# Three low bits of a narrowed weight: from a shift on VectorE to an activation on ScalarE

## The chip, the core and the metric

The kernel runs on one core of one Trainium2 chip. The metric is device time in microseconds (us) of one execution; lower is better. A core has TensorE (PE, with a separate row PEld for its weight loads), VectorE (DVE), ScalarE (ACT), GpSimd (POOL) and SyncE (SP), each with its own instruction stream that it works through in order. Here SP issues most DMAs, ACT a few, and POOL only sets up constants.

## The reference, cut to what matters

```python
# attention, batch 8, heads 8, 576 rows, head size 64, 32 packed queries
p_packed = sm_attn(p, k, v)               # softmax attention of p over k, v
out = sm_attn(q, p_packed, p_packed)      # q over the packed rows
x = out.transpose(0, 2, 1, 3).reshape(4608, 512)
h = maximum(maximum(x @ w1, x @ w2), x @ w3)   # 512 -> 768
x = h @ w_out                                   # 768 -> 512
h = x @ w_in2                                   # 512 -> 2048
g = maximum(h, 0) + log1p(exp(-abs(h)))
return g @ w_out2                               # 2048 -> 512
```

The weight matrices arrive as 64-bit floats; q, k, v and p arrive as 32-bit floats. The kernel reads each 64-bit number as two 32-bit words, the low word first.

## The kernel before, in words

**Stages.** The program works through eight batches. For each it runs the packed attention (q and k transposed, scores, exponentials, a transposed copy, the value products), then layer 1 (`layer1_unit`, L397: 18 units of 12 matmuls per batch, the maximum over three weights), then layer 2 (`layer2`, L434). The last part (`layer3`, `layer4`, from L814) runs the two large layers over nine chunks of 512 rows. Every fp32 product is made of three matmuls on a high and a low part, which `split` (L105) makes: L106 on ScalarE rounds to the high part, L107 on VectorE subtracts it.

**Narrowing.** A 64-bit weight is brought to fp32 by two helpers. `rebase` (L79) takes the high word as a float and moves its exponent with one ScalarE activation (L82). `narrow` (L90) takes the top three bits of the low word with a VectorE shift in place (L93), and then shifts the rebased bits left by three and ors these bits in (L96, VectorE). It is called 56 times on a tile of 128 x 512: 18 times for the three layer 1 weights (`narrow_w`, tiles `wraw` to `wsb`), 6 times for the layer 2 weight (`split_wo`, tiles `woraw` to `wo32`), and 32 times for the weights of the last two layers (`narrow_ahead`, L639, tiles `raw` to `x32`), which are stored narrowed and read back later. The first 24 stand in the first 105 us; the other 32 are spread over batches 1 to 6, six slots per batch.

**What sets the order.** The first batch is written as a string of step names (L490 to L499), where `LWfw` loads a layer 1 weight, `Nfw` narrows it, `LOf` and `SOf` do the same for the layer 2 weight, `S`, `E`, `Vv`, `PT`, `A` are the steps of the attention, and `PW` is the product of packed rows and weights (`ps_w`, L374). A scheduler then places the instructions of each engine by its own estimate of when their inputs are there, so the order on an engine is not that of the string. In the later batches TensorE's units are chained (`pinned`, L568) and SP's loads too (`in_turn`, L625). The raw weight tiles come from a pool of 5 buffers (`stp`), q and k tiles from a pool of 5 (`rx`), PSUM tiles of the attention stages from a pool of 4 (`mm`). A load of a sixth weight waits until an earlier tile has been narrowed by L96.

**Names used below.** `woraw_204` is the second layer 2 weight tile; `wraw_597` is the eleventh layer 1 weight tile to be loaded. `mx` (L261) is the row maximum of the first scores, `e` (L270) their exponential, `e1T` (L291) the copy of its transpose, `ps_v` (L305) the value products, `pp` (L319) the packed rows that result, `ps_t` (L230) their transpose, `ps_s` (L246) the scores, and `s` (L332) the transposed scores of the second softmax.

Of the kernel before, what the change touches and what calls it, by code (L numbers as in the profile page):

```python
# [11 lines left out]
AF = mybir.ActivationFunctionType  # L12
ALU = mybir.AluOpType
# [6 lines left out]
def packed_attention_maxout_softplus(  # L20
# [22 lines left out]
    nc = tc.nc  # L43
# [46 lines left out]
    def narrow(raw, x):  # L90

        low, bits = raw[:, :, 0], x.bitcast(I32)
        nc.vector.tensor_scalar(  # L93
            out=low, in0=low, scalar1=29, scalar2=None, op0=ALU.logical_shift_right
        )
        nc.vector.scalar_tensor_tensor(  # L96
            out=bits,
            in0=bits,
            scalar=3,
            in1=low,  # L100
            op0=ALU.logical_shift_left,
            op1=ALU.bitwise_or,
        )
# [31 lines left out]
    praw, raw, vt, pT, e1, esum, e1T, pp, ppT = ({} for _ in range(9))  # L135
# [328 lines left out]
    def split_wo(f, t):  # L464
        x = mp.tile([P, S], F32, tag="m", name="wo32")
        rebase(t, x[:, :DM])
        narrow(t, x[:, :DM])
        split(x[:, :DM], wo_hi[:, f], wo_lo[:, f])
# [11 lines left out]
    def narrow_w(f, w, t):  # L480
        x = wsb[:, 3 * f + w].rearrange("p c x -> p (c x)")
        rebase(t, x)
        narrow(t, x)
# [155 lines left out]
    def narrow_ahead():  # L639
        if len(in_flight) == AHEAD or not to_narrow and in_flight:  # L640
            raw64, dst = in_flight.pop(0)
            x = nwp.tile([P, 512], F32, tag="x32", name="x32")
            rebase(raw64, x)
            narrow(raw64, x)
            if len(dst.shape) == 3:
                x = x.rearrange("p (j x) -> p j x", x=P)
            to_store.append((dst, x))
        if to_narrow:
            src, dst = to_narrow.pop(0)
            t = stp.tile([P, 512, 2], I32, tag="st", name="raw64")  # L650
            in_turn(lambda: nc.sync.dma_start(out=t.rearrange("p n t -> p (n t)"), in_=src))
            in_flight.append((t, dst))
# [294 lines left out]
```

## Time and profile before

| | |
|---|---|
| runs without a profile | 1292.54, 1289.27, 1292.12 us; median 1292.12 |
| the profiled execution | 1288.91 us, of which the span from first to last instruction is 1287.1 |
| PE busy | 1250.0 us (97%), 9952 matmuls |
| PEld busy | 1127.7 us (88%) |
| DVE busy | 719.4 us (56%), 1115 instructions |
| ACT busy | 458.2 us (36%), 669 instructions |
| chain that ended last | PE 81%, DVE 2%, DMA 1% of the span |

All times of the profile are of that one execution, counted from its first instruction. Busy shares are means over stages that differ much: PE's row of 40 slices begins 3, 8, 8 and then stays at 9 or more. So the first slices and the rest have to be read apart, and in the first slices what matters is what each engine waited for.

### The profile page before, as it was taken

What the parts mean: (1) busy time and instruction counts of PE and PEld (TensorE: products, weight loads), DVE (VectorE), ACT (ScalarE), POOL (GpSimd) and SP (SyncE); (2) the same over time, 40 slices, a digit from 0 to 9 for tenths busy, and PEclk for the clock granted to TensorE, in tenths of its full rate; (3) what the DMA queues carried; (4) which work ended last, traced back from release to release, by engine and by line L of the source; (5) the groups of instructions that cost most, each with busy time, mean ns of one, the idle gap of its engine ahead of it and who ended that gap; (6) DMA issues with size and microseconds to landing.
All of it is one profiled execution on the core that took longest, in us unless ns stands there. A gap on an engine that the chain in (4) does not pass through costs nothing.

```text
span 1287.1 us, 23495 instructions
## 1 busy us (share of the span) xinstructions
PE 1250.0 (97%) x9952; PEld 1127.7 (88%) x9952; DVE 719.4 (56%) x1115; ACT 458.2 (36%) x669; POOL 0.7 (0%) x6
## 2 busy tenths in 40 slices
PE   3889999999999999999999999999999999999998
PEld 2679898998989899999999999999999999999997
DVE  3777777786857657686354443544434445444332
ACT  3553434444343434553323323232232222332221
POOL 0000000000000000000000000000000000000000
PEclk7899999999999999999999999999999999999999
DMA  9972848677685724977646556565465554654651
GB/s 263 240 212 91 204 136 231 174 212 193 185 231 171 201 87 166 343 257 266 225 172 225 187 208 214 187 215 212 180 208 203 205 205 172 228 188 180 213 182 58
DMA packets 82121, 255.10 MB, mean 198 GB/s; under 512 B 12128, under 2 KB 47200, under 8 KB 72544
## 3 DMA queue, kind: packets, MB, share of 16 engines
q1 hardware_dynamic: 76240, 242.46, 59.1%
q10 hardware_dynamic: 5776, 11.14, 2.5%
q8 instruction: 78, 1.28, 0.4%
q14 instruction: 27, 0.22, 0.1%
HBM read 211.62 MB, written 41.94 MB: 197 GB/s over the span
## 4 chain that ended last, share of the span: by engine, by line
PE 81%; DVE 2%; DMA 1%; issue 0%; ACT 0%; SPq 0%; DVEq 0%
PE ps L812 28%; PE ps L395 21%; PE acc L860 10%; PE acc L859 10%; PE acc L858 10%; PE ps_w L374 2%; DMA wc<-wic 1%; PE ps_v L305 1%; PE ps_e L285 1%; DVE pwlo L107 1%; DVE mx L261 0%; PE ps_s L246 0%; DVE m L420 0%; DVE x L96 0%; DMA qraw<-in_q_dram 0%
## 5 line engine op out<-in xcount | busy, mean ns | idle before, releaser
L812 PE MATMUL ps<-x2hi,wc 128*128 128x256 f32 x2016 | 370.6, 282 | 0.8 <-DMA wc<-wic 0.8
L812 PEld LDWEIGHTS ps<-x2hi,wc 128*128 128x128 f32 x2016 | 316.1, 190 | 3.9 <-DMA wc<-wic 1.3
L812 PE MATMUL ps<-x2lo,wc 128*128 128x256 f32 x1008 | 283.7, 281 | 0.0
L860 PE MATMUL acc<-w2hi,glo 128*128 128x512 f32 x576 | 224.9, 391 | 0.0
L859 PE MATMUL acc<-w2lo,ghi 128*128 128x512 f32 x576 | 224.8, 390 | 0.0
L858 PE MATMUL acc<-w2hi,ghi 128*128 128x512 f32 x576 | 224.3, 389 | 0.0
L812 PEld LDWEIGHTS ps<-x2lo,wc 128*128 128x128 f32 x1008 | 191.4, 190 | 2.8
L841 ACT ACTIVATE h<-h 128x1024 f32<-128x1024 f32 x72 | 76.3, 1059 | 286.3 <-DVE h L838 286.3
L835 DVE TENSOR_TENSOR h<-h,ps 128x512 f32<-128x512 f32 x72 | 49.5, 687 | 227.8 <-PE ps L812 227.8
L107 DVE TENSOR_TENSOR glo<-h,ghi 128x1024 fp32r<-128x1024 f32 x72 | 88.1, 1223 | 85.1 <-ACT ghi L106 85.0
L395 PE MATMUL ps<-a2hi,pwhi 128*128 128x288 f32 x576 | 129.2, 306 | 2.9 <-DVE pwlo L107 0.9
L860 PEld LDWEIGHTS acc<-w2hi,glo 128*128 128x128 f32 x576 | 108.1, 188 | 23.0 <-DVE glo L107 0.2
L858 PEld LDWEIGHTS acc<-w2hi,ghi 128*128 128x128 f32 x576 | 108.3, 188 | 20.3
L859 PEld LDWEIGHTS acc<-w2lo,ghi 128*128 128x128 f32 x576 | 108.1, 188 | 20.5
L395 PE MATMUL ps<-a2lo,pwhi 128*128 128x288 f32 x576 | 123.8, 297 | 0.3 <-DVE a2lo L107 0.3
L395 PE MATMUL ps<-a2hi,pwlo 128*128 128x288 f32 x576 | 123.6, 296 | 0.0
L395 PEld LDWEIGHTS ps<-a2hi,pwhi 128*128 128x128 f32 x576 | 91.8, 189 | 17.9 <-ACT m L418 5.9
L834 ACT ACTIVATE h<-ps 128x256 f32<-128x256 f32 x72 | 27.5, 382 | 188.0 <-PE ps L812 188.0
L420 DVE TENSOR_TENSOR m<-ps,m 128x576 f32<-128x576 f32 x96 | 72.4, 755 | 38.8 <-PE ps L395 31.4
L395 PEld LDWEIGHTS ps<-a2lo,pwhi 128*128 128x128 f32 x576 | 93.1, 190 | 0.6 <-DVE a2lo L107 0.5
L395 PEld LDWEIGHTS ps<-a2hi,pwlo 128*128 128x128 f32 x576 | 93.0, 190 | 0.2 <-DVE pwlo L107 0.2
L107 DVE TENSOR_TENSOR pwlo<-ps_w,pwhi 128x512 fp32r<-128x512 f32 (+1 forms) x80 | 50.5, 631 | 67.1 <-ACT pwhi L106 66.6
(87 smaller groups left out, 1473.8 us busy)
## 6 DMA issues: line engine op xcount, KB each, us to landing
wc<-wic SPq DMA_DIRECT2D x66, 1792.0 KB
qraw<-in_q_dram SPq DMA_DIRECT2D x112, 140.0 KB
wic<-wc SPq DMA_DIRECT2D x8, 1792.0 KB
kraw<-in_k_dram SPq DMA_DIRECT2D x96, 140.0 KB
wraw<-in_moe_w_dram SPq DMA_DIRECT2D x18, 512.0 KB
x2d<-xs ACTq DMA_DIRECT2D x32, 288.0 KB
xu<-x2d SPq DMA_DIRECT2D x36, 256.0 KB
out_dram<-o SPq DMA_DIRECT2D x136, 64.0 KB
```

The lines of the kernel that those rows point to most:

```text
L107: nc.vector.tensor_tensor(out=lo, in0=src, in1=hi.bitcast(F32), op=ALU.subtract)
L285: nc.tensor.transpose(ps[: 32 * TI, i // hi, (i % hi) * P : (i % hi) * P + P], e[:, i], ident,)
L374: nc.tensor.matmul(ps[cols, G, : units * P].rearrange("p (w x) -> p w x", w=units), ppT[n][rows, cols], wsb[rows, 4 * c : 4 * c + units, g ...
L395: nc.tensor.matmul(o, w, xx, start=first, stop=last)
L420: nc.vector.tensor_tensor(out=m, in0=ps[:, :, :HS], in1=ms[n, f], op=ALU.max)
L812: nc.tensor.matmul(out, l, r, start=(i == 0), stop=(i == len(terms) - 1))
L834: nc.scalar.activation(out=h[:, 3], in_=pa[:, 0], func=AF.Copy)
L835: add(out=h[:, 0:5:4], in0=h[:, 3:4].to_broadcast([P, 2, HC]), in1=pb, op=ALU.add)
L841: nc.scalar.activation(out=g, in_=g, func=AF.Softplus)
L858: nc.tensor.matmul(ps, ghi[:, i, cols], whi, start=first, stop=False)
L859: nc.tensor.matmul(ps, ghi[:, i, cols], wlo, start=False, stop=False)
L860: nc.tensor.matmul(ps, glo[:, i, cols], whi, start=False, stop=last)
```

## The change

In `narrow`, the VectorE shift of the low word by 29 is gone. In its place ScalarE reads the top byte of the low word (every eighth byte of the tile) as an unsigned 8-bit number b, computes b/32 - 31/64, and writes it as a 32-bit integer back to the low word's place. [...] L96 on VectorE then reads the word as before; its other input still comes from L82 on ScalarE.

```diff
     def narrow(raw, x):
 
         low, bits = raw[:, :, 0], x.bitcast(I32)
-        nc.vector.tensor_scalar(
-            out=low, in0=low, scalar1=29, scalar2=None, op0=ALU.logical_shift_right
-        )
+        top = raw.bitcast(mybir.dt.uint8)[:, :, 3]
+        nc.scalar.activation(out=low, in_=top, func=AF.Copy, scale=1.0 / 32, bias=-31.0 / 64)
         nc.vector.scalar_tensor_tensor(
             out=bits,
```

56 VectorE instructions leave and 56 ScalarE instructions (L94 of the changed kernel) come. Every later line of the changed kernel has a number one lower than before (L96 is its L95). Because the scheduler places instructions anew, others move too.

VectorE, around 30 us, between the narrowing of `wraw_199` and of `wraw_211`, before:

```order
L96 SCALAR_TENSOR_TENSOR wsb_114<-wsb_114,wraw_199 128x512
L93 TENSOR_SCALAR woraw_204<-woraw_204 128x512
L261 TENSOR_REDUCE mx_283<-ps_s_265 128x1
L96 SCALAR_TENSOR_TENSOR wo32_255<-wo32_255,woraw_204 128x512
L265 TENSOR_SCALAR ms_285<-mx_283 128x1
L261 TENSOR_REDUCE mx_290<-ps_s_266 128x1
```

The same place of VectorE in the changed kernel:

```order
L95 SCALAR_TENSOR_TENSOR wsb_114<-wsb_114,wraw_199 128x512
L260 TENSOR_REDUCE mx_283<-ps_s_265 128x1
L260 TENSOR_REDUCE mx_290<-ps_s_266 128x1
L95 SCALAR_TENSOR_TENSOR wo32_255<-wo32_255,woraw_204 128x512
L264 TENSOR_SCALAR ms_285<-mx_283 128x1
```

Both maxima now stand ahead of everything that needs the tile `woraw_204`; the scaling of the first maximum (L265, now L264) still stands behind its L96.

ScalarE, at the same place, before (from the rebase of `woraw_204` to the second `e1T`):

```order
L82 ACTIVATE wo32_255<-woraw_204 128x512
L211 ACTIVATE vT_237<-ps_k_238 128x3x3x32 x2
L232 ACTIVATE pT_302<-ps_t_300 128x128
L106 ACTIVATE wo_hi_115<-wo32_255 128x512
L270 ACTIVATE e1_287,es_288<-ps_s_265,ms_285 128x576
L82 ACTIVATE wsb_114<-wraw_211 128x512
L270 ACTIVATE e1_294,es_295<-ps_s_266,ms_292 128x576
L291 ACTIVATE e1T_311<-ps_e_304 96x768
L82 ACTIVATE wsb_114<-wraw_216 128x512
L291 ACTIVATE e1T_323<-ps_e_316 96x768
```

ScalarE there in the changed kernel, from the new instruction on `woraw_204`:

```order
L94 ACTIVATE woraw_204<-woraw_204 128x512
L231 ACTIVATE pT_302<-ps_t_300 128x128
L105 ACTIVATE wo_hi_115<-wo32_255 128x512
L82 ACTIVATE wsb_114<-wraw_211 128x512
L94 ACTIVATE wraw_211<-wraw_211 128x512
L269 ACTIVATE e1_287,es_288<-ps_s_265,ms_285 128x576
L269 ACTIVATE e1_294,es_295<-ps_s_266,ms_292 128x576
L82 ACTIVATE wsb_114<-wraw_216 128x512
L94 ACTIVATE wraw_216<-wraw_216 128x512
L290 ACTIVATE e1T_311<-ps_e_304 96x768
L82 ACTIVATE wsb_114<-wraw_221 128x512
L94 ACTIVATE wraw_221<-wraw_221 128x512
```

The second `e1T` follows directly behind these rows. Four new instructions and two rebases that stood elsewhere are now between the rebase of `woraw_204` and the second `e1T`.

VectorE, around 80 us, where the packed rows `pp` of batch 1 are made, before:

```order
L107 TENSOR_TENSOR hlo_876<-m_828,hhi_875 128x576
L107 TENSOR_TENSOR pwlo_851<-ps_w_852,pwhi_850 128x512
L96 SCALAR_TENSOR_TENSOR wsb_114<-wsb_114,wraw_870 128x512
L319 TENSOR_SCALAR pp_880<-ps_v_879,rc_931 128x64
L107 TENSOR_TENSOR pwlo_851<-ps_w_852,pwhi_850 128x512
L319 TENSOR_SCALAR pp_880<-ps_v_879,rc_936 128x64
L107 TENSOR_TENSOR wo_lo_116<-wo32_943,wo_hi_115 128x512
```

The same place in the changed kernel:

```order
L95 SCALAR_TENSOR_TENSOR wsb_114<-wsb_114,wraw_870 128x512
L106 TENSOR_TENSOR hlo_876<-m_828,hhi_875 128x576
L95 SCALAR_TENSOR_TENSOR wo32_943<-wo32_943,woraw_779 128x512
L106 TENSOR_TENSOR pwlo_851<-ps_w_852,pwhi_850 128x512
L106 TENSOR_TENSOR wo_lo_116<-wo32_943,wo_hi_115 128x512
L318 TENSOR_SCALAR pp_880<-ps_v_879,rc_931 128x64
L318 TENSOR_SCALAR pp_880<-ps_v_879,rc_936 128x64
L106 TENSOR_TENSOR pwlo_851<-ps_w_852,pwhi_850 128x512
```

The first `pp` now stands behind the whole narrowing and splitting of the third layer 2 weight (`woraw_779`), the second no longer behind the second `pwlo`. On SP, the loads of one k tile of batch 1 and of `wraw_597` now stand ahead of the load of v for batch 1 (`vt`), which waits for `ps_v` of batch 0; `wraw_597` stood behind eight loads of q before. On TensorE, in the first two units of layer 1, matmuls of the second unit on the first head group now stand between the two head groups of the first unit. From batch 1 on, the order is the same but for the moved instructions themselves and a few neighbours.

## Rows read from the trace of the kernel before

**Rows 1.** Stretches: us; busy PE, PEld, DVE, ACT, POOL; clock, DMA share, GB/s.
```profile
0.00:57.40 57.40, 33.53 (x533) 24.67 (x533) 27.99 (x57) 25.40 (x48) 0.70 (x6) 0.79 1.02 254
57.40:69.30 11.90, 10.11 (x75) 9.53 (x75) 9.41 (x21) 5.87 (x12) 0.00 (x0) 1.00 0.42 138
69.30:82.60 13.30, 9.26 (x171) 7.21 (x172) 12.60 (x25) 9.12 (x16) 0.00 (x0) 1.00 0.90 250
90.00:515.00 425.00, 422.74 (x4279) 382.09 (x4278) 304.10 (x527) 176.87 (x307) 0.00 (x0) 1.00 0.64 176
515.00:1275.00 760.00, 759.17 (x4825) 690.69 (x4824) 359.88 (x482) 238.10 (x285) 0.00 (x0) 1.00 0.58 207
```

**Rows 2.** PE's longest wait from 90 to 515 us: total, times, longest.
```profile
PE ps L395 <- DVE pwlo L107: 0.9, 5, 0.2
```

**Rows 3.** Groups of one shape: busy us, mean ns | idle before, releaser.
```profile
L93 DVE TENSOR_SCALAR raw<-raw 128x512 int32<-128x512 int32 x32 | 13.2, 413 | 0.0
...
L93 DVE TENSOR_SCALAR wraw<-wraw 128x512 int32<-128x512 int32 x18 | 7.6, 421 | 17.9 <-DMA wraw<-in_moe_w_dram 17.9
...
L93 DVE TENSOR_SCALAR woraw<-woraw 128x512 int32<-128x512 int32 x6 | 2.5, 423 | 2.3 <-DMA woraw<-in_moe_w_out_dram 2.3
...
L82 ACT ACTIVATE wsb<-wraw 128x512 f32<-128x512 f32 x18 | 12.0, 681 | 17.7 <-DMA wraw<-in_moe_w_dram 17.6
...
L106 ACT ACTIVATE wo_hi<-wo 128x512 fp32r<-128x512 f32 x6 | 3.8, 629 | 0.5 <-DVE wo L96 0.5
...
L841 ACT ACTIVATE h<-h 128x1024 f32<-128x1024 f32 x72 | 76.3, 1059 | 286.3 <-DVE h L838 286.3
```

**Rows 4.** Timeline of ACT: start, duration, instruction, count, idle before.
```profile
30.38 0.68 ACT L211 ACTIVATE vT<-ps_k 128x288 f32<-128x288 f32 x2
...
32.06 0.72 ACT L270 ACTIVATE e<-ps_s,ms 128x576 f32<-128x576 f32 x1
...
35.77 0.81 ACT L291 ACTIVATE e1T<-ps_e 96x768 f32<-96x768 f32 x1
```

**Rows 5.** Timeline of ACT from 60 to 70 us.
```profile
64.60 0.65 ACT L418 ACTIVATE m<-ps 128x576 f32<-128x576 f32 x1 [0.78 <-PE ps L395]
65.15 1.23 ACT L82 ACTIVATE wsb<-wraw 128x512 f32<-128x512 f32 x2
```

**Rows 6.** Timeline of DVE from 26 to 37 us.
```profile
29.80 0.43 DVE L93 TENSOR_SCALAR woraw<-woraw 128x512 int32<-128x512 int32 x1 [2.07 <-DMA woraw<-in_moe_w_out_dram]
30.14 0.75 DVE L261 TENSOR_REDUCE mx<-ps_s 128x1 f32<-128x576 f32 x1
30.81 0.68 DVE L96 SCALAR_TENSOR_TENSOR wo<-wo,woraw 128x512 int32<-128x512 int32 x1
```

**Rows 7.** Timeline of DVE from 35 to 46 us.
```profile
38.52 0.48 DVE L319 TENSOR_SCALAR pp<-ps_v,rc 128x64 f32<-128x64 f32 x2 [0.64 <-PE ps_v L305]
...
44.57 1.45 DVE L332 STREAM_TRANSPOSE s<-ps_s 128x576 f32<-128x576 f32 x2 [1.92 <-PE ps_s L246]
```

**Rows 8.** Timeline of PE from 35 to 59 us.
```profile
35.66 2.79 PE L305 MATMUL ps_v<-vt,e1T 96*32 96x64 f32 x96
...
57.41 0.53 PE L395 MATMUL ps<-a2hi,pwhi 128*128 128x288 f32 x2 [0.60 <-ACT a2hi L106]
58.20 0.52 PE L395 MATMUL ps<-a2lo,pwhi 128*128 128x288 f32 x2 [0.27 <-DVE a2lo L107]
```

**Rows 9.** Timeline of PE from 69 to 83 us.
```profile
69.28 1.09 PE L374 MATMUL ps_w<-wsb,ppT 64*32 64x512 f32 x16 [1.52 <-DVE wsb L96]
...
76.93 1.09 PE L374 MATMUL ps_w<-wsb,ppT 64*32 64x512 f32 x16 [0.98 <-DVE wsb L96]
...
82.56 0.30 PE L230 MATMUL ps_t<-ident,pp 128*128 128x128 f32 x1 [3.06 <-DVE pp L319]
```

**Rows 10.** Timeline of SP from 31 to 52 us: issues.
```profile
31.52 0.37 SPq L472 DMA_DIRECT2D wraw<-in_moe_w_dram  x1
38.51 0.33 SPq L169 DMA_DIRECT2D vt<-in_v_dram  x1
```

## The prediction, written before the changed kernel ran

> **What bounds the kernel now.** The table of stretches comes first, because the kernel has two parts. From 90 to 515 us PE is busy 422.74 of 425.00 us, and from 515 to 1275 us 759.17 of 760.00, both at the full granted clock, 1.00 or 2.4 GHz [rows 1]. There PE is the bound. In PE's list of waits for the first of these stretches the largest entry is 0.9 us, in five pieces of at most 0.2 [rows 2]. The 32 narrowings of batches 1 to 6 lie here: whatever they save or cost on other engines, PE hardly waits for them. Before 90 us it is otherwise: up to 57.4 us PE works 33.53 of 57.40 us, while the DMA engines are full (share 1.02); from 57.4 to 69.3 it works 10.11 of 11.90; and from 69.3 to 82.6 only 9.26 of 13.30, while VectorE is busy 12.60 [rows 1]. So the time of the kernel is decided by when PE comes out of this beginning. I then read, in the timelines, each PE wait there: 0.60 and 0.27 us for the split of the second softmax at 57.41 and 58.20 [rows 8], and then 1.52 for a narrowed weight at 69.28, 0.98 for another at 76.93, and 3.06 for the packed rows `pp` at 82.56 [rows 9]. After the last PE never stops for long.
>
> **The change part by part.** Removed: 56 shifts of VectorE, 13.2 + 7.6 + 2.5 = 23.3 us, 0.42 us each [rows 3]. 32 of them (13.2 us) lie beside a PE that is the bound and are worth nothing. 24 (10.1 us) lie before 105 us.
>
> Added: 56 activations of 128 x 512 on ScalarE. No row shows one that reads a byte. The nearest is L82, which reads the same tile in the same step of eight bytes: 681 ns, of which a neighbour behind it overlaps some, two in a row taking 1.23 us or 0.61 each [rows 3, 5]. From below I take 629 ns, the same size read without a step (L106), and from above 1059 ns, an activation of 1024 elements (L841), as if each byte cost two [rows 3]. I take 0.68, or 0.61 in a row, since tile, size and step are those of L82. Could it be a gain? Not on ScalarE, where nothing leaves.
>
> Page rule and row differ a little here. L82 against L106 shows 0.05 us for the step [rows 3]. The Trainium skill (SBUF — State Buffer, the passage on cachelines) says that accesses run at full rate as long as at least two fall on one 16-byte line. A byte from every eight has two, so by it the instruction would take the 629 ns of L106, and the sum below would be 0.5 instead of 1.1 us.
>
> The late part: 32 x 0.61 = 20 us more on ScalarE, which has 176.87 of 425.00 us of work there [rows 1]; what hides it is PE's own work. I put it at nothing. If the cover were gone, as with a copy of `pp` delayed by one instruction, it would cost up to 0.6 us for each of six batches, 3.6 us.
>
> The first place, 30 to 58 us. Before, the first maximum (L261) waits on VectorE behind a shift that waits for the DMA of `woraw_204`, until 29.80 us [rows 6]. The shift gone, the maximum moves ahead by about 2 us. But this gain isn't kept: the scaling of the maximum still stands behind L96 of that tile, which now waits for ScalarE. From the landing at 29.80, ScalarE has L82 (0.61), two L211 (0.68 together [rows 4]) and the new instruction (0.61); L96 takes 0.68 [rows 6]: 32.4. Then come the split's high part (0.6), L82 and the new one (1.2), two exponentials (0.72 each [rows 4]), L82 and the new one (1.2), the first `e1T` (0.7, an 0.81 instruction less overlap), L82 and the new one (1.2), the second `e1T`, 0.81: it ends at 32.4 + 7.1 = 39.5, against 36.6 before (35.77 + 0.81 [rows 4]), 2.9 later. The second half of `ps_v` follows (half of 2.79 [rows 8]), to 40.9; a fifth new instruction holds the L96 ahead of `pp` until 41.4; so `pp` starts 2.8 us later than its 38.52 [rows 7], and with it the transposes of q and the scores. A sixth (on `wraw_597`, now loaded earlier) stands among the copies of the transposed q, some 0.3 us that count. The softmax of q starts at 47.7 instead of 44.57 [rows 7], 3.1 later. From there to 57.41 nothing new stands in the chain, and the new order takes 0.2 less. PE's new order lets it do nine matmuls of the first two units without the waits of 0.60 and 0.27 us [rows 8]; I count 0.5. So layer 1 starts 3.1 - 0.2 - 0.5 = 2.4 us late.
>
> The second place, 64 to 83 us. `wraw_597` is loaded and narrowed early now: SP put its load behind v, which waited from 31.89 to 38.51 us [rows 10], and it no longer does. So the narrowing at 69.28 needs one tile fewer, and the 1.52 us of PE's wait there [rows 9] nearly go: the product starts at 70.1, only 0.8 late. But then ScalarE is the chain. From the copy L418 (64.60 before [rows 5], 67.0 now) to the second-last split before `pp`, its new order has seven L82 (0.60 each, 4.2), eight new ones (0.60, 4.8), two L418 (1.1), two splits of 576 (1.2), three of 512 (1.6) and an `e1T` (0.7): 13.6, with some 0.8 of waits for VectorE, to 81.4 us. Then VectorE has, ahead of `pp`, one split's low part, the narrowed `woraw_779` split, and `pp` itself: 2.2 us in all. `ps_t` starts at 83.6 instead of 82.56 [rows 9]. Behind it PE has work for the rest, so this 1.1 us is the sum.
>
> The profiled execution took 1288.9 (its span 1287.1 and 1.8 around it): 1290.0. The median of the runs shown is 3.2 higher; I forecast on that: 1292.1 + 1.1 = 1293.2 us.
>
> **The rivals.** *The new instruction is dear.* Six stand in the first chain and eight in the second, so each 0.1 us over 0.68 costs 1.4. At 1059 ns that is 14 x 0.38 = 5.3 more, 6.4 in all, 1298.5. It decides from 0.88 us: there the sum passes 3.9. For it: no row shows a byte input written as an integer in place. Against it: L82 is nearly the same access. A rule points the same way: the Trainium skill (ScalarE: Activation LUTs, "Rules for kernel authors") gives plain arithmetic to VectorE; the rows agree on this size, 0.42 against 0.68 [rows 3], and if all 24 differences of 0.26 stood in series they would cost 6.2 us, 1298.3.
>
> *VectorE's relief wins.* In the stretch to 82.6 us VectorE is the fuller engine (12.60 against 9.12 of 13.30 [rows 1]), and a wait of a shift on a DMA no longer blocks it. If ScalarE's additions all fell into its pauses, PE could win the 2 us of the maximum and the 1.52 and 0.98 at the narrowed weights: 4.5 us, 1287.6. Against it: the order puts the new instructions ahead of the exponentials and both `e1T`, not into pauses.
>
> *The beginning is bound by DMA.* With a share of 1.02 up to 57.4 us [rows 1], a slip of the engines may only use time in which the next tile hadn't landed: no change, 1292.1. For it: L93 waited 17.9 us in all for weights [rows 3]. Against it: SP waits for `ps_v` before it goes on [rows 10], so a late `ps_v` delays the loads too.
>
> **How the numbers follow.** A difference under 0.3%, 3.9 us, is about what a measurement of this kernel can't tell from none; the runs shown differ by 3.3. Forecast 0.60, DMA-bound 0.15, dear instruction 0.17, VectorE's relief 0.08. So faster 0.08, the same 0.75, slower 0.17. The forecast's own range is 1290 to 1297: above by the 3.6 us of a late part without cover, below by the 3.2 us that the profiled execution lies under the median. The range reaches to the dear instruction's 1298 above and to 1288, short of the relief's 1287.6, below.
>
> **What would show it.** L94 at 0.63 to 0.72 us, 56 of them; `e1T` for the second time near 38.7 us; the softmax of q (L332's successor) near 47.7; the wait at the product that now stands near 70 us gone but for 0.1 to 0.3; `ps_t` of batch 1 near 83.6; PE's busy share from 90 to 515 us as before. The forecast is wrong if `ps_t` starts before 81 or after 86, if L94 takes over 0.88 us, or if PE's idle time after 90 us grows by more than 2 us.

## The result: 0.54% slower, in the range but six times the predicted loss

The changed kernel takes 1296.3 us (median of 9 runs, 1293.35 to 1299.98). The kernel before, timed beside it, takes 1290.18 (9 runs, 1288.54 to 1293.53). The ratio is 1.0054, with a 95% interval of 1.0043 to 1.0066: slower by 7.0 us (the two medians lie 6.1 apart). The range of 1288 to 1298 holds the time by luck: it was built on a median of 1292.1, and built on the 1290.18 measured here it would have ended at 1296.1. The loss itself was forecast at 1.1 us, "the same", and it is 7.0; by the 0.3% that the prediction itself set as the line, the result is "slower", to which it gave 0.17, for another reason. Two executions among the kernels below took far longer (2054.01 us in experiment 1, at a granted clock of 0.563, and 3807.88 in experiment 10) and enter no ratio, and the only trace of experiment 1 is of that execution and is not read.

The profiled execution of the changed kernel took 1298.54 us, with a span of 1296.7. That is 2.2 above its median, so not all of its 9.6 us over the span before is the change. The stretches, to be held against [rows 1] (the same windows and columns):

```profile
0.00:57.40 57.40, 33.83 (x514) 25.89 (x521) 20.10 (x39) 31.19 (x59) 0.70 (x6) 0.94 1.01 259
57.40:69.30 11.90, 9.36 (x73) 8.39 (x59) 9.71 (x21) 5.11 (x10) 0.00 (x0) 0.86 0.46 155
69.30:82.60 13.30, 12.04 (x147) 9.97 (x149) 8.86 (x13) 10.85 (x20) 0.00 (x0) 1.00 0.54 163
90.00:515.00 425.00, 421.73 (x4262) 381.04 (x4262) 290.16 (x488) 192.60 (x340) 0.00 (x0) 1.00 0.63 173
515.00:1275.00 760.00, 757.69 (x4814) 690.02 (x4813) 362.63 (x484) 239.32 (x285) 0.00 (x0) 1.00 0.59 211
```

VectorE gives up 7.9 us in the first 57.4 us (27.99 to 20.10) and ScalarE takes 5.8 (25.40 to 31.19). PE is as busy there as before, but its matmul count falls by 19: the same busy time holds less work. That is a hint, and no more, that it ran at a lower clock; the clock column speaks against it (0.94, against 0.79 before), and the durations below have to decide.

The new instruction itself, by shape (columns as in [rows 3]):

```profile
L95 DVE SCALAR_TENSOR_TENSOR wsb<-wsb,wraw 128x512 int32<-128x512 int32 x18 | 12.4, 690 | 32.0 <-ACT wraw L94 31.9
L94 ACT ACTIVATE raw<-raw 128x512 int32<-128x512 uint8 x32 | 21.6, 676 | 0.0
L94 ACT ACTIVATE wraw<-wraw 128x512 int32<-128x512 uint8 x18 | 11.9, 661 | 0.0
L94 ACT ACTIVATE woraw<-woraw 128x512 int32<-128x512 uint8 x6 | 3.8, 660 | 0.2 <-DMA woraw<-in_moe_w_out_dram 0.2
```

It takes 0.66 to 0.68 us, no more than L82 on the same tile. VectorE, which waited 17.9 us for these weights at L93 before [rows 3] and 4.6 more at L96, now waits 32.0 us ahead of L95, nearly all of it for L94: the 7.6 us that it saved on these tiles turned into waiting.

PE from 34 to 88 us (start, duration, instruction, count, idle before), to be read beside [rows 8, 9]:

```profile
37.72 0.99 PE L304 MATMUL ps_v<-vt,e1T 96*32 96x64 f32 x48
39.34 0.88 PE L304 MATMUL ps_v<-vt,e1T 96*32 96x64 f32 x48 [0.63 <-ACT e1T L290]
41.68 0.45 PE L229 MATMUL ps_t<-ident,pp 128*128 128x128 f32 x1 [1.46 <-DVE pp L318]
42.05 6.03 PE L197 MATMUL ps_k<-ident,qraw 96*64 96x96 f32 x72
...
59.38 0.53 PE L394 MATMUL ps<-a2hi,pwhi 128*128 128x288 f32 x2 [1.30 <-ACT a2hi L105]
60.58 0.53 PE L394 MATMUL ps<-a2lo,pwhi 128*128 128x288 f32 x2 [0.66 <-DVE a2lo L106]
...
61.93 1.30 PE L394 MATMUL ps<-a2hi,pwhi 128*128 128x288 f32 x4 [0.57 <-DVE pwlo L106]
63.03 0.68 PE L394 MATMUL ps<-a2lo,pwhi 128*128 128x288 f32 x2
...
73.04 1.09 PE L373 MATMUL ps_w<-wsb,ppT 64*32 64x512 f32 x16
...
80.97 1.09 PE L373 MATMUL ps_w<-wsb,ppT 64*32 64x512 f32 x16 [1.25 <-DVE wsb L95]
...
87.61 0.45 PE L229 MATMUL ps_t<-ident,pp 128*128 128x128 f32 x1 [4.08 <-DVE pp L318]
87.72 0.83 PE L394 MATMUL ps<-a2hi,pwhi 128*128 128x288 f32 x2
88.34 0.68 PE L394 MATMUL ps<-a2lo,pwhi 128*128 128x288 f32 x2
```

And the same transposes of q, before the change:

```profile
39.37 3.19 PE L198 MATMUL ps_k<-ident,qraw 96*64 96x96 f32 x72
```

The 72 transposes take 6.03 us in place of 3.19. The granted clock says why (PE busy, clock, DMA share, GB/s):

```profile
38.00:40.00 2.00, 1.37 (x96) 1.00 1.10 271
40.00:42.00 2.00, 0.54 (x17) 0.86 0.68 186
42.00:44.00 2.00, 2.00 (x25) 0.50 1.01 243
44.00:46.00 2.00, 2.00 (x30) 0.50 1.10 216
46.00:48.00 2.00, 2.00 (x27) 0.50 1.11 224
48.00:50.00 2.00, 1.90 (x36) 0.94 1.16 260
```

In 40 to 42 us PE works only 0.54 of 2.00; the clock falls from 1.00 to 0.50, that is from 2.4 to 1.2 GHz, and stays there until 48 us. It falls again at two more places. Behind the waits of 1.30, 0.66 and 0.57 us at the start of layer 1 the pairs of L394 take 0.68 us instead of 0.42 until 65.4: from 61.93 to 65.39 PE needs 3.46 us for what takes 1.91 in experiment 5, where they stay fast, as they do in the kernel before. And behind the 4.08 us wait at 87.61 they take 0.68 again. One warning on this column: it reads 1.00 where durations show half speed (the first `ps_e` matmuls of this kernel, 0.23 us each against 0.14 later). The duration of a known instruction is the safer witness.

The bookkeeping of this one execution, as the lead that the kernel before has over it at landmarks: `pp` 2.5 us (41.06 against 38.52), softmax of q 5.5 (50.08 against 44.57), product near 70 us 3.8 (here the 1.52 us wait of before is gone), `ps_t` of batch 1 5.05, first layer 2 copy 5.7 (113.92 against 108.21), last one 6.8 (535.88 against 529.05). The large layers add 2.8, where PE waited 2.3 us for the first block of weights in place of 0.8 and then ran slowly for a moment. In another execution of nearly the same program (the fourth experiment) that wait was 0.4, so I leave this term out; without it the profile agrees with the median.

The growth from 5.7 to 6.8 over seven batches is mostly one short wait in each of four of them (PE's waits from 90 to 515 us, to be read beside [rows 2]):

```profile
PE ps L394 <- DVE pwlo L106: 2.4, 5, 0.6
```

ScalarE there, near 315 us: L94 now stands between the two high-part splits, which were 1.36 us apart before and are 1.61 apart now.

```profile
314.88 0.60 ACT L105 ACTIVATE pwhi<-ps_w 128x512 fp32r<-128x512 f32 x1 [1.46 <-PE ps_w L373]
315.37 0.68 ACT L94 ACTIVATE raw<-raw 128x512 int32<-128x512 uint8 x1
315.94 0.66 ACT L82 ACTIVATE x<-raw 128x512 f32<-128x512 f32 x1
316.49 0.59 ACT L105 ACTIVATE pwhi<-ps_w 128x512 fp32r<-128x512 f32 x1
```

### The profile page after: what moved, and what is told of

Its sections match the earlier page's. It is cut to its first block, busy times and chain, and to the rows that moved or that the text cites. A ratio compares the mean times of both kernels' runs of the same rounds, so it can differ in the third digit from the quotient of the medians.

```text
span 1296.7 us, 23471 instructions
## 1 busy us (share of the span) xinstructions
PE 1255.4 (97%) x9952; PEld 1133.5 (87%) x9952; DVE 701.1 (54%) x1059; ACT 487.5 (38%) x725; POOL 0.7 (0%) x6
## 4 chain that ended last, share of the span: by engine, by line
PE 89%; DMA 4%; DVE 4%; ACT 2%; SPq 1%; issue 1%; DVEq 0%
PE ps L811 27%; PE ps L394 27%; PE acc L859 10%; PE acc L858 10%; PE acc L857 10%; PE ps_w L373 2%; DMA woraw<-in_moe_w_out_dram 1%; DMA wc<-wic 1%; DMA qraw<-in_q_dram 1%; PE ps_e L284 1%; PE ps_s L245 1%; PE ps_v L304 1%; DVE pwlo L106 1%; DVE mx L260 1%; DVE m L419 1%
## 5 line engine op out<-in xcount | busy, mean ns | idle before, releaser
L394 PE MATMUL ps<-a2hi,pwhi 128*128 128x288 f32 x576 | 130.0, 308 | 5.1 <-DVE pwlo L106 3.0
L394 PE MATMUL ps<-a2lo,pwhi 128*128 128x288 f32 x576 | 124.2, 298 | 0.7 <-DVE a2lo L106 0.7
L394 PE MATMUL ps<-a2hi,pwlo 128*128 128x288 f32 x576 | 124.4, 298 | 0.0
L394 PEld LDWEIGHTS ps<-a2hi,pwhi 128*128 128x128 f32 x576 | 93.0, 192 | 20.1 <-ACT m L417 5.9
L394 PEld LDWEIGHTS ps<-a2lo,pwhi 128*128 128x128 f32 x576 | 93.8, 191 | 0.9 <-DVE a2lo L106 0.9
L394 PEld LDWEIGHTS ps<-a2hi,pwlo 128*128 128x128 f32 x576 | 93.6, 191 | 0.2 <-DVE pwlo L106 0.2
```

The costliest lines, as they stand in the source:

```text
L394: nc.tensor.matmul(o, w, xx, start=first, stop=last)
```

## The experiments

Most of them choose for each narrowing whether ScalarE or VectorE takes the bits:

```diff
-    def narrow(raw, x):
+    def narrow(raw, x, on_act=True):
...
+        if on_act:
+            nc.scalar.activation(out=low, in_=top, func=AF.Copy, scale=1.0 / 32, bias=-31.0 / 64)
+        else:
+            nc.vector.tensor_scalar(out=low, in0=low, scalar1=29, ..., op0=ALU.logical_shift_right)
```

All ratios are to the kernel before, run beside each on the same chip; 0.001 is 1.3 us.

| | kernel | median us | ratio, 95% interval | q's transposes, us | first layer 2 copy at |
|---|---|---|---|---|---|
| | changed kernel | 1296.3 | 1.0054, 1.0043 to 1.0066 | 6.03 | 113.92 |
| 1 | 32 late narrowings alone | 1290.65 | 1.0006, 0.9990 to 1.0021 | | |
| 2 | 24 early ones alone | 1292.87 | 1.0035, 1.0024 to 1.0047 | 5.95 | 112.17 |
| 3 | first 12 alone | 1289.90 | 1.0007, 0.9997 to 1.0018 | 3.19 | 105.68 |
| 4 | changed, matmuls ahead of `ps_e` | 1296.28 | 1.0054, 1.0039 to 1.0068 | 6.03 | 114.61 |
| 5 | changed, batch 0's gaps filled | 1295.01 | 1.0048, 1.0030 to 1.0066 | 3.19 | 109.40 |
| 6 | changed, both batches' gaps filled | 1291.50 | 1.0022, 1.0010 to 1.0034 | 3.19 | 107.44 |
| 7 | before, gaps filled | 1290.86 | 1.0013, 1.0000 to 1.0025 | 3.2 | 108.30 |
| 8 | all but the first 12 | 1291.71 | 1.0016, 1.0001 to 1.0032 | 3.19 | 110.07 |
| 9 | the third again | 1290.38 (1 run) | | 4.84 | 108.46 |
| 10 | changed, `wo` behind `pp` | 1294.97 | 1.0031, 1.0017 to 1.0044 | 6.03 | 113.30 |
| 11 | before, `wo` behind `pp` | 1291.20 | 1.0011, 0.9996 to 1.0026 | 6.03 | 109.76 |
| 12 | 24 early ones, both gaps filled | 1289.85 | 0.9997, 0.9986 to 1.0008 | 3.19 | 110.49 |

The last two columns are of one profiled execution each, and the beginning shifts from one execution to the next (in the kernels with the longer chain, the first exponential starts at 32.34 to 34.13 us), so they are read with care. The traces of runs 3, 5 and 6 are of the fastest execution of each, 4.4, 2.0 and 2.7 us under the median.

**1. The late 32 alone** (`on_act=False` in `narrow_w` and `split_wo`).

> The ScalarE form only in the 32 narrowings of batches 1 to 6; the first 24 as before. Theory A (the loss of 6 us is made before 90 us): the beginning is that of before, ps_t of batch 1 near 82.6 us; what stays is PE's longer wait for pwlo in batches 2 to 6 (0.55 instead of 0.18 us), 1 to 2 us in all, ratio to before 1.000 to 1.002. Rival B (the loss comes from the 32 later ones, through waits for pwlo and a later start of the large layers): ratio 1.003 to 1.006.

Ratio 1.0006 with 1 inside the interval, which reaches to 1.0021: alone, they cost nothing that can be told.

**2. The early 24 alone** (`on_act=False` in `narrow_ahead`).

> The ScalarE form only in the first 24 narrowings; the 32 later ones as before. Theory A: ps_t of batch 1 near 87.6 us as in the changed kernel, ratio 1.003 to 1.005. Rival B: ratio under 1.002.

1.0035: the larger part of the loss is made in the first 105 us. PE from 36 us, where the waits are shorter than in the changed kernel and the transposes slow all the same:

```profile
40.36 0.44 PE L234 MATMUL ps_t<-ident,pp 128*128 128x128 f32 x1 [0.84 <-DVE pp L323]
40.74 5.95 PE L202 MATMUL ps_k<-ident,qraw 96*64 96x96 f32 x72
```

**3. The first twelve alone** (`(f, w) < (3, 1)` in `narrow_w`, `f < 2` in `split_wo`, none late), up to `pp` of batch 0 the same instructions as in the second.

> The ScalarE form only in the first 12 tiles (wraw 00 to 30 and the first two woraw), all others on VectorE. If the first chain (from the landing of the second woraw at 30 us to the softmax of q) sets the loss: softmax of q near 50 us, ps_t of batch 1 near 86 to 87, ratio 1.003 to 1.004. If the second chain (the eight new instructions between 66 and 88 us) sets it: ps_t of batch 1 back to 83 to 84.5, ratio under 1.002.

1.0007: the first chain by itself doesn't make the loss, though its profile has `pp` 6.95 us after the first exponential, like the second experiment's 6.92. In this execution, the fastest of twelve, the clock did not fall at the transposes (it did at the start of layer 1, where pairs take 0.68 us until 59.2):

```profile
39.91 0.30 PE L234 MATMUL ps_t<-ident,pp 128*128 128x128 f32 x1 [0.92 <-DVE pp L323]
40.13 3.19 PE L202 MATMUL ps_k<-ident,qraw 96*64 96x96 f32 x72
...
45.23 2.20 PE L202 MATMUL ps_k<-ident,kraw 96*64 96x96 f32 x48
...
67.71 1.09 PE L378 MATMUL ps_w<-wsb,ppT 64*32 64x512 f32 x16
```

The last two lines show where a late `pp` is made good: the kernel before waits there for a k tile (the line below) and 1.52 us for a narrowed weight [rows 9]; here PE waits for neither.

```profile
47.77 1.25 PE L198 MATMUL ps_k<-ident,kraw 96*64 96x96 f32 x24 [2.09 <-DMA kraw<-in_k_dram]
```

**4. PE warmed earlier**: 16 matmuls of the identity in the 5.9 us gap ahead of the first `ps_e`.

```diff
+        for _ in range(16 if (n, G) == (0, 0) else 0):
+            nc.tensor.matmul(ps[:, 0, :P], ident, ident, start=True, stop=True)
```

> The changed kernel with 16 more matmuls on the identity (128x128, about 0.3 us each, overwritten afterwards) where PE waits for the first exponential, 29 to 35 us; nothing else moves on ScalarE or VectorE. If the low granted clock from 41.5 to 48.5 us follows from PE's idle 5.9 us at 29 to 35: the clock stays at 1.0 there, the three transposes of q take 3.2 instead of 6.0 us, the softmax of q starts near 47.2 instead of 50.1, ratio to before 1.002 to 1.004. If the fall has another cause (the sparse transposes before, or nothing in the kernel): the transposes still take 6 us and the ratio stays at 1.0054.

1.0054, as without. The first `ps_e` now run at full speed (12 in 1.47 us instead of 2.80), but the clock falls at 42 us as before. Work ahead of the earlier gap did not help here; the gaps right before the transposes were left, as this run's timeline of PE shows:

```profile
40.16 0.88 PE L306 MATMUL ps_v<-vt,e1T 96*32 96x64 f32 x48 [0.95 <-ACT e1T L292]
42.50 0.45 PE L229 MATMUL ps_t<-ident,pp 128*128 128x128 f32 x1 [1.46 <-DVE pp L320]
42.88 6.03 PE L197 MATMUL ps_k<-ident,qraw 96*64 96x96 f32 x72
```

**5. Those gaps filled** (`K` = 5 in `attn1_values` and 9 ahead of `ps_t` in `transpose_p`; the trace has two records for each).

```diff
+            for _ in range(5 if (n, G) == (0, 1) else 0):
+                nc.tensor.matmul(ps[:, 1, P : 2 * P], ident, ident, start=True, stop=True)
...
+        for _ in range(fill):
+            nc.tensor.matmul(ps[:, 1, :P], ident, ident, start=True, stop=True)
```

> The changed kernel with idle TensorE time of the first batch filled: 5 matmuls of the identity between the two halves of the first batch's ps_v, and 9 between ps_v and ps_t, where the trace of the changed kernel has gaps of 0.63 and 1.46 us. Nothing else differs. Theory K (the 72 transposes of q run at half the clock, 6.03 us in place of 3.19, because of the idle time that the change lets in ahead of them): transposes back at about 3.2 us, ps_t of the first batch at most 0.4 us later, the layers 2.5 us earlier, ratio to the kernel before 1.003 to 1.004 (changed kernel: 1.0054). Rival L (the time is only handed to the next wait, which the late chain of VectorE and ScalarE sets): transposes short, but the first matmul of layer 1 no earlier than 59 us, ratio 1.005 or more. Rival M (the low clock comes from something else than this idle time): transposes stay at 6.0 us, ratio 1.005 to 1.006.

PE in this run's timeline, from the filling to batch 1's `ps_t` (columns as above):

```profile
40.01 2.27 PE L230 MATMUL ps_t<-ident 128*128 128x128 f32 x18
42.12 0.27 PE L231 MATMUL ps_t<-ident,pp 128*128 128x128 f32 x1
42.32 3.19 PE L197 MATMUL ps_k<-ident,qraw 96*64 96x96 f32 x72
...
56.81 0.53 PE L398 MATMUL ps<-a2hi,pwhi 128*128 128x288 f32 x2 [1.29 <-ACT a2hi L105]
...
83.28 0.45 PE L231 MATMUL ps_t<-ident,pp 128*128 128x128 f32 x1 [4.85 <-DVE pp L322]
```

The trace is as theory K has it: 3.19 us at the transposes, layer 1 at 56.81. The filling holds `ps_t` up itself, by 1.2 us against the first `ps_e` (7.88 after it, 6.69 in the changed kernel), more than the 0.4 expected. Of the time, part goes to a longer wait for `pp` of batch 1, 4.85 us, as rival L has it. The ratio of 1.0048 lies between K's number and L's, and its interval takes in both: by the time alone it is undecided.

Nor is it true that nothing else differs. Up to the end of the transposes only one rebase and its L94 have moved on ScalarE, so the 3.19 belongs to the filling. Later the order of several instructions on ScalarE and VectorE, and of loads on SP, is another than in the changed kernel (the load of one layer 2 weight is issued at 72.92 us instead of 79.84). The same holds for run 6, for run 12 against run 2, and for run 7 against the kernel before. So their times are those of a filling and a new order together.

**6. Both batches' gaps filled** (20 more ahead of batch 1's `ps_t`).

> As the run with the first batch's gaps filled, and 20 more matmuls of the identity ahead of the second batch's ps_t, where the changed kernel's TensorE waits 4.08 us for pp and then runs about 5 us at half the clock (ps_t 0.45 us, pairs of L394 0.68 us apiece in place of 0.42). Theory K: ps_t 0.30 us, the pairs behind it 0.42 from the start, another 2 us less: ratio 1.001 to 1.0025. Rival L: ratio no more than 0.0005 below that of the run with the first batch alone filled. Rival M: pairs stay at 0.68 for 5 us, and the added matmuls cost up to 1 us: ratio as the other run's or 0.001 above it.

PE behind batch 1's filling, in this run's timeline:

```profile
83.32 0.33 PE L231 MATMUL ps_t<-ident,pp 128*128 128x128 f32 x1 [1.09 <-DVE pp L322]
83.40 0.51 PE L398 MATMUL ps<-a2hi,pwhi 128*128 128x288 f32 x2
83.75 0.42 PE L398 MATMUL ps<-a2lo,pwhi 128*128 128x288 f32 x2
```

1.0022, within K's numbers; the pairs take 0.42 us from the second on. Up to 90 us the order on ScalarE and VectorE is that of run 5, and from `ps_t` of batch 1 to the next product PE takes 9.85 us instead of 12.13: the half clock cost 2.3 us there, in line with the 0.0026 between the two ratios.

With matmuls that compute nothing, more than half of the loss is gone (1.0054 to 1.0022, 4 us). Experiments 2 and 12 differ by the same filling and agree: 1.0035 to 0.9997, 4.9 us. That all of this was PE's clock is not shown, since the order changed too, and since the filling also speeds up pairs behind `ps_t` that run slowly in the kernel before as well (about 1.5 us).

**7. The kernel before, filled** (5 and 16).

> The kernel before (shift on VectorE) with the same filling, sized to its own gaps: 5 matmuls of the identity ahead of the first batch's ps_t (gap 0.69 us) and 16 ahead of the second batch's (gap 3.06 us). Theory K: q's transposes run at full speed there already, so the first filling gives nothing; of the second batch's first pairs of L395, seven take 0.68 us in place of 0.42, so 1.5 to 1.8 us go: ratio 0.9985 to 0.999. If K does not hold for the second gap, or the added matmuls delay ps_t: 1.000 to 1.001. If this is the fastest of all, the change is not needed for it.

1.0013: a miss for K, no gain. The pairs behind `ps_t` do run at 0.42 us, but in this execution the clock fell one wait earlier:

```profile
76.71 1.92 PE L376 MATMUL ps_w<-wsb,ppT 64*32 64x512 f32 x16 [2.18 <-DVE wsb L96]
```

The product takes 1.92 us in place of 1.09 behind a wait of 2.18 [rows 9: 0.98]. The order of the narrowings on VectorE changed with the filling, so this wait may come from the order; a clean counter-test it is not.

**8. All but the first twelve** (the third experiment's complement).

> ScalarE takes the bits only of the wide tiles from the fourth group of first weights on, of woraw from the third on, and of the 32 late narrowings; the first twelve tiles keep VectorE's shift. The first chain is then as before: second e1T 36.7 us, pp 38.5, q's transposes 3.2 us. Theory K, every place pays for its own: second batch's ps_t waits 1 us longer than the 3.06 of before, its slow stretch is 1 to 2 us longer, the late pwlo waits add 1.5 us: ratio 1.002 to 1.0035. Rival N (the second place makes the whole loss): 1.0045 or more. Rival O (the loss is the clock fall after the first chain alone): 1.001 or less.

1.0016 [1.0001 to 1.0032]: N (1.0045) is out; K (1.002 to 1.0035) and O (1.001) both lie in the interval. From the first `ps_t` to the second it takes 44.41 us against 43.41 before, the 1 us that was expected, and eleven pairs behind it run slowly instead of seven.

**9. The third again, one execution.**

> The kernel of the first chain alone once more (ScalarE in the first twelve narrowings), for a second profile of it. In its first profile the second e1T, pp and ps_t came as late as in the kernel with all 24 early narrowings on ScalarE, and yet q's 72 transposes took 3.19 us there and 5.95 us in the other. If the fall of the clock follows from the chain alone (theory K, strict): 3.2 us again, since the chain is the same. If an execution can go either way with the same gaps (theory K, loose): 3.2 or 6.0 us, and a 6.0 here would show it; the run's time is then some 3 us above the 1285.5 of the first profile.

PE in this run's timeline, three of the rows of the third:

```profile
41.06 0.30 PE L234 MATMUL ps_t<-ident,pp 128*128 128x128 f32 x1 [1.46 <-DVE pp L323]
41.30 4.84 PE L202 MATMUL ps_k<-ident,qraw 96*64 96x96 f32 x72
...
70.50 1.09 PE L378 MATMUL ps_w<-wsb,ppT 64*32 64x512 f32 x16
```

The same program: 4.84 us here, 3.19 there. `ps_t` still ran at full speed and the clock fell within the transposes. So an execution can go either way with the same instructions. The Trainium skill (TensorE: Matmul & The Clock Gate, "Part 1: The HAM clock gate") says of the start of a kernel that the number of its slow matmuls varies from run to run. These two executions show the like in the middle of one.

The pair also shows what the slow transposes cost, with no instruction changed. `ps_t` starts 1.15 us later here and the transposes take 1.65 longer, 2.80 together; the product near 70 us comes 2.79 later (70.50 against 67.71) and the first layer 2 copy 2.78. So behind the longer chain, time lost at the transposes reaches layer 2 in full.

**10. `wo` behind `pp`**: one line of the table of steps.

```diff
-        LW50 N50 N42 PW3 LW51 N51 LW52 N52 L1S2 Vv1 PT1 SO2 L13 LO3 SO3 L14 PW4 L1S3
+        LW50 N50 N42 PW3 LW51 N51 LW52 L1S2 Vv1 PT1 N52 L13 SO2 LO3 SO3 L14 PW4 L1S3
```

> The changed kernel with one line of its table of steps in another order: the narrowing of the fifteenth wide tile of first weights and the split of the third wo tile come after the second batch's packed transpose. On VectorE the wo addition and wo_lo, 0.69 us each, no longer stand ahead of the second batch's pp, and on ScalarE L82, wo_hi and L94 of wo go; one pwlo comes ahead of pp instead. Theory Q (the second batch's pp is late because of what stands ahead of it on the two engines): pp and ps_t 0.7 to 1.5 us earlier against the first batch's ps_t (45.9 us between the two in the changed kernel), ratio 1.004 to 1.005 (changed kernel: 1.0054). Rival R (pp waits for its inputs, or the time is handed to later narrowings): ratio 1.0055 or more.

The time (1.0031) is better than theory Q asked, but the trace doesn't show its reason: from `ps_t` to `ps_t` 45.67 us against 45.93, 0.26 less in place of 0.7 to 1.5. The second `pwlo`, now ahead of `pp`, waits 0.66 us for ScalarE in the place that was won. The intervals of the two ratios overlap, so I take nothing from this run.

**11. The same in the kernel before.**

> The kernel before with the same line of its table in the other order: three operations of 0.69 us (wo's addition, one wsb addition, wo_lo) no longer stand ahead of the second batch's pp on VectorE, but a shift of woraw and the second pwlo come ahead of it, and wo's L82 and wo_hi go from ScalarE. Theory Q: ps_t of the second batch 0.3 to 1 us earlier, ratio 0.999 to 1.000. Rival R: 1.000 to 1.001.

1.0011, no difference that can be told. Its trace has the more useful row: with the first chain of the kernel before, which the edit doesn't touch, the transposes were slow here.

```profile
37.53 0.45 PE L230 MATMUL ps_t<-ident,pp 128*128 128x128 f32 x1 [0.69 <-DVE pp L319]
37.91 6.03 PE L198 MATMUL ps_k<-ident,qraw 96*64 96x96 f32 x72
```

And this execution took 1289.84 us, 0.9 more than the profiled one of before, with no wait for a k tile behind the transposes (2.09 us there); the product near 70 us starts at 69.34, against 69.28. In the kernel before, a fall at this place is paid by that wait; in the changed kernel, where the k tile has long landed, it is not.

**12. The early 24 on ScalarE, both gaps filled, the late 32 on VectorE.**

> ScalarE in the first 24 narrowings only (VectorE keeps the 32 late shifts), and both of the first two batches' gaps filled with identity matmuls (5, 9 and 20). It puts together what the earlier runs took apart: the low clock gone by the filling, the late waits for pwlo (2.4 us with the change, 0.9 without) gone by VectorE's late shifts. Theory K (the loss is the low clock in two places, the second chain, and 1.5 us of late waits): 1 to 2 us below the filled kernel with all 56 on ScalarE (ratio 1.0022): 1.0005 to 1.0015, so no faster than the kernel before, since the second chain's lateness remains. If the late part costs nothing: 1.002 again. If the filling frees a gain of VectorE's relief: under 1.000, and it is the fastest version.

0.9997 [0.9986 to 1.0008]: the loss is gone, but nothing is gained. The pairs at the start of layer 1 are slow here too (0.69 us), so even this kernel pays for the clock at one place. PE's waits from 90 to 515 us:

```profile
PE ps L403 <- DVE pwlo L111: 1.1, 6, 0.2
```

Against the sixth experiment (2.6 us in 6) the late waits are 1.5 us shorter; the ratio falls by 0.0025, 3.2 us, which is more than these waits show, but the two intervals leave room for 1.5. No version tried beats the kernel before by what can be told.

## Why the prediction was right, and where its size was wrong

- **L94's duration: right.** 0.66 to 0.68 us for the 0.68 taken from L82. The byte read costs what L82 costs at the same step of eight bytes, and not the 629 ns that follow from the Trainium skill's passage on cachelines (SBUF — State Buffer); the difference over 24 narrowings is under 1 us. The dear instruction is out.
- **The first chain to `pp`: right.** `e1T` ends the second time at 39.28 (39.5 forecast), `pp` starts at 41.06 (41.3). The sum had the order right: of the rebases only that of `wraw_221` newly stands ahead of the second `e1T`, not two as told with the change.
- **From `pp` to the softmax of q: this step failed.** "So `pp` starts 2.8 us later than its 38.52, and with it the transposes of q and the scores" took them over at their old 3.19 us. They took 6.03, and the softmax began 5.5 us late, not 3.1. So PE's work at half its clock was put at nothing, and it is 2.84 us here. Runs 5, 6 and 12 show the gaps behind it: with these filled, 3.19 in three of three. Runs 3 and 9 show that the loss is passed on in full. Of the profiles with the longer first chain and these gaps unfilled, four have about 6.0, one 4.84 and one 3.19; of three with the old chain and none, one has 6.03.
- **"I count 0.5" for the waits of the first two units: wrong in sign.** The waits of 0.60 and 0.27 [rows 8] became 1.30, 0.66 and 0.57, and behind them PE lost 1.55 us more at half its clock (3.46 against run 5's 1.91).
- **The wait of 1.52 at the weight near 70 us goes: right, but bought nothing.** The product starts at 73.04 without a wait, not at 70.1, because everything before it was later.
- **ScalarE as the second chain: right, and its length nearly.** From the copy L417 (69.94, forecast 67.0) to the end of the second-last split (85.30) it took 15.4 us instead of 14.4; a wait of 1.12 us for a weight's DMA is in it. `ps_t` came at 87.61 instead of 83.6: 2.9 us from the late start and 1.1 from this chain and the 2.3 us behind it (2.2 forecast). It lies past the 86 us that the prediction named as its own refutation. The third sign is passed too: PE's idle time after 90 us grew by 2.5 us in this execution (2.26 + 0.83 before, 3.27 + 2.31 now), 1.5 of it the wait at the large layers.
- **"Behind it PE has work for the rest, so this 1.1 us is the sum": wrong.** Behind a wait of 4.08 us PE had work at half its clock. Its first ten pairs took 4.93 us (87.72 to 92.65) instead of 4.25 (82.62 to 86.87), 0.7 more. The kernel before runs slowly here too, so the 2.3 us that filling this gap gives (run 6 against run 5) are not all the change's.
- **The late part at nothing: too low.** The prediction had the mechanism as its upper bound, an instruction between two copies, at up to 3.6 us. In the changed kernel it is 1.5 us of waits (2.4 against 0.9). In the ratios it is 0.0006 alone, but 0.0019 on top of the early 24 (changed kernel against run 2) and 0.0025 with filled gaps (run 6 against 12), 2 to 3 us.
- **The other rivals.** VectorE's relief: it waits 31.9 us for L94, so there was no pause to win; the kernel comes level only with filled gaps and without the late part (run 12), and whether the relief gives anything there is not shown. The beginning bound by DMA: not with a loss of 7 us, but the k tile's wait does hide a single lateness (runs 3 and 11).

The parts don't add up: the first twelve alone cost 0.9 us, the late 32 alone 0.8, all but the first twelve 2.1, and all together 7.0. The traces suggest one reason: a single lateness falls into waits that the kernel before has anyway, 2.09 us for the k tile and 1.52 for the weight; those are used up once. What of the 7.0 us is shown: the slow transposes (2.84 us in the trace, passed on in full in runs 3 and 9), the late start of `pp` (2.5) and the late waits (1.5). ScalarE's second chain and the half clock at the other two places add to these, and the 1.52 us wait that is gone takes from them; how much each is worth is argued from single traces. Open stays why the clock falls in one execution and not in another of the same program, and how often it does in either kernel: that needs many profiles of each. Also open is the part of the 3.2 us between runs 6 and 12 that the late waits don't explain.

## What to carry to other kernels

Moving work off an engine that waits onto one that stands in a dependent chain can lengthen the chain, however the totals look; here VectorE gave up 10.1 us in the first 24 narrowings and got waiting. When a change opens gaps ahead of TensorE, take the matmuls behind each gap at the duration they have at the lower clock as one end of the range, since a gap of 1.5 us was followed by 6 us at half speed. And look for the waits that the old kernel has behind the place: here they took up one lateness, and there was nothing left for a second. Last, where a scheduler places the instructions, filling a gap also changes their order: compare the order on every engine before the time is put down to the filling alone.

## What the runs showed of the hardware

- After gaps of 0.63 and 1.46 us the granted clock went to 0.50 for about 6 us, 41.5 to 48 us, though PE was fully busy in that time. Matmuls that compute nothing, put into the gaps, kept the speed (72 transposes in 3.19 us); the same ahead of an earlier gap did not (one profile).
- The length of the last gap doesn't decide it: 0.84 us and slow (run 2), 0.92 and fast (run 3), 0.69 and fast (before) or slow (run 11).
- The clock column can read 1.00 while the matmuls run at half speed: in run 2 it does so from 14 to 60 us, with q's transposes at 5.95 us within.
- A ScalarE activation that reads one byte of every eight and writes integers in place took 661 ns on 128 x 512, as one on 32-bit words at the same step (668).
